# Two paddings of 32 bytes in SBUF ahead of the expert buffers of a fused attention and mixture-of-experts kernel

## The chip, the cores and the metric

The kernel runs on one core of one Trainium2 chip. The metric is the device time of one execution in microseconds (us), median of three runs.

## The reference, cut to what matters

```python
# attention: B=4, H=8, S=768, D=64; 4 sink keys and a window of 128, causal
scores = np.where(is_sink | in_window, q @ k.T / 8, -1e9)
x = softmax(scores) @ v                  # turned to (N=3072, DM=512)
# mixture of experts: E=8, F=1024, each token goes to its top 2 experts
noisy = x @ w_gate + log1p(exp(x @ w_noise)) * noise
top2, top2_w = two largest of noisy, softmax over the two
for e in range(8):
    h = relu(x[rows of e] @ w1[e])       # 512 -> 1024
    out[rows of e] += top2_w * (h @ w2[e])   # 1024 -> 512
```

All inputs and the output are float32.

## The kernel before, in words

The first stage is attention. It takes 16 pairs of heads one after the other; keys and queries of a pair land in a ring of three buffers `kq`. Scores are matmuls of line 600 into PSUM, ACT takes the exponentials into `cbuf`, TensorE transposes them (line 657), ACT or DVE copies them to `CT` (POOL makes the masked copy `CM`), and lines 682 and 685 multiply them by the values. The results are transposed, scaled and written to `x_rows` in HBM; the router (`logits`, `routing`) picks the experts meanwhile.

The second stage computes the experts one after the other on up to 832 (experts 0 to 3) or 768 rows each. Every float32 operand is split into a high and a low part (both float32r), and a product is three matmuls: high by high, high by low, low by high.

- Expert 0 multiplies up in lines 1259 to 1261 (stationary `wr`, and `hb` for the last quarter; moving `xe`, 512 columns, and `hb`, 320 columns) and down in lines 1530 to 1536.
- Experts 1 to 7 multiply up by a scheme with seven products for eight, lines 1660 to 1662 in `seven`. The stationary operand is a block of 128 columns of the weights in `wr`. The moving operand is a block of rows of 416 columns (experts 1 to 3) or 384 (4 to 7). The low parts of the rows (line 1661), and the high parts of the last products, lie in `x7`, which the profile writes as `x`; the high parts of the first four products lie in `xe`. `hb` takes the result.
- They multiply down in line 1691 (1694 for a half tile), `down7`. The stationary operand is a block of 128 columns of `hb`; the moving operand is a block of 512 columns of the weights `w2`. Chunks 0 and 1 of these weights (parts f = 0 to 3 of the sum) lie in `w2a`, chunks 2 and 3 (f = 4 to 7) in `w2b`.

Each of these matmuls loads its own stationary operand (PEld). The weights come from HBM into the ring `st`; ACT writes the high part (lines 1331 and 1372) and DVE the low part (line 503). Rows are gathered by POOL's indirect DMAs into `sg`, loaded to `xg` and transposed by DVE (line 1414). Results leave with an accumulating indirect DMA (line 1554).

Every engine's order is a list written out by hand (`ORDER` for the attention, `ORDER2` for the experts), so none of it depends on what a tile's address is. A few matmuls of `one` by itself (bfloat16, line 1961) fill TensorE's time before the experts.

Tiles are placed pool by pool, one behind the other, each rounded up to 32 bytes of a partition. The pools stand in the order `consts` (entered first, small tables), `early` (`st`, `wr`, `w2a`, `sg`, `xg`, `xe`), `tail` (tables, `turned`, `strip`, `ri`, `lg`), and then the attention's own pools (`cbuf`, `kq`, `CT` and others), whose place the experts' pool `msb` (`tmp`, `x7`, `hb`, `w2b`) takes later. `experts_setup` allocates the last tiles of `consts` (lines 1162 to 1171); the tile `turned` of `tail` is allocated in `moe_kernel`, line 1977. The program's allocation lists these first bytes, here with what is left of a division by 128:

| tile | first byte | over a multiple of 128 |
|---|---|---|
| `one`, `idf` | 8320, 9344 | 0 |
| `st`, `wr`, `w2a`, `sg`, `xg`, `xe` | 12896, 21088, 49760, 66144, 70496, 74848 | 96 |
| `turned`, `strip`, `tmp`, `x7`, `hb`, `w2b` | 96832, 112192, 116032, 123456, 156736, 212032 | 64 |
| `kq`, three buffers | 131520, 137760, 144000 | 64, 32, 0 |
| `cbuf`, `pcbuf`, `vr`, `CT`, `CM`, `ps` | 117760, 130432, 156672, 164864, 175104, 174080 | 0 |
| `vn` | 150240 | 96 |

The blocks that one expert matmul reads lie at multiples of 128 bytes from their tile's first byte (512 bytes for a stationary block, 1664 from one block of rows to the next, 2048 for `w2`, 6912, 3584 and 512 in `hb`), so all blocks of a tile stand over a multiple of 128 by the same number as the tile.

Of the kernel before, what the change touches and what calls it, by code (L numbers as in the profile page):

```python
# [9 lines left out]
F32 = mybir.dt.float32  # L10
# [399 lines left out]
def view(region, o, shape, dt):  # L410

    n = math.prod(shape[1:]) * (2 if dt in (F16, BF) else 4) // 4
    x = region[:shape[0], o:o + n].bitcast(dt)
    if len(shape) < 3:
        return x
    names = "abcd"[:len(shape) - 1]
    return x.rearrange(f"p ({' '.join(names)}) -> p {' '.join(names)}", **dict(zip(names, shape[1:])))
# [71 lines left out]
def constants(nc, pool, sh):  # L489
    c = {}  # L490
    c["one"] = pool.tile([128, 128], BF, name="one")
    nc.vector.memset(c["one"], 1.0)
    c["nz"] = pool.tile([128, sh.T, sh.E], F32, name="nz")
    jp = c["nz"].rearrange("p t e -> p (t e)")[:, :128].bitcast(I32)
    nc.gpsimd.iota(jp, pattern=[[1, 128]], base=0, channel_multiplier=-1)
    c["idf"] = pool.tile([128, 128], F32, name="idf")
    nc.vector.tensor_scalar(c["idf"], jp, 0.0, None, op0=OP.is_equal)
    c["jp"] = jp
    return c
# [369 lines left out]
def gate_loads(nc, plan, cst, sh, w_gates, noise):  # L869
    c, wbd = cst, cst["wbd"]  # L870

    def load():
        nc.sync.dma_start(wbd.rearrange("p g h i e -> p (g h i e)"), w_gates)
        nc.sync.dma_start(c["nz"].rearrange("p t e -> p (t e)"), noise)

    c["gates"] = lambda: plan.dma(2, load, 2.5, r=[("xrow", 0)], w=[("rc", 0)], n=2)
# [285 lines left out]
def experts_setup(nc, cst, sh, pool):  # L1162
    c = cst
    c["idg"] = pool.tile([128, sh.TE], I32, name="idg")
    c["idx"] = pool.tile([128, sh.E, sh.TE], I32, name="idx")
    c["at"] = {}
    c["own"] = pool.tile([128, 4], F32, name="own")
    nc.vector.tensor_tensor(c["own"], c["io"][:, :4], c["quad"].to_broadcast([128, 4]), op=OP.is_equal)
    c["pick"] = [pool.tile([128, 4, sh.E], F32, name=f"pick{i}") for i in range(2)]
    c["spacer"] = pool.tile([1, 1], F32, name="spacer")  # L1170
    c["wc"] = [pool.tile([128, sh.TE], F32, name=f"wc{i}") for i in range(2)]


def row_tile(sh, e, t):
# [720 lines left out]
def banks(*regions):  # L1895
    held = {}

    def get(i, shape, dt):
        if shape is not None:
            held[i] = view(regions[i % len(regions)], 0, shape, dt)  # L1900
        return held[i]

    return get
# [20 lines left out]
def carried(plan, sh):  # L1924
    return [(kx, plan.wrote[kx][-1]) for kx in [("lgs", (sh.B - 1) * sh.S // 256 + i) for i in range(sh.S // 256)] + [(x, 0, t) for x in ("xh", "xl") for t in range(sh.FA)]]


def phase_two(tc, nc, plan, cst, sh, w1, w2, xbuf, out):

    b, NT = sh.B - 1, sh.S // 128  # L1930
    plan.rings.update(lg=1, lt=1, lm=1, old=1, X=1, h=9)

    def turned():
        nc.gpsimd.iota(plan.get("y", -3, [128, 128], F32).rearrange("p (s i) -> p s i", i=4), pattern=[[1, 32], [32, 4]], base=0,
                       channel_multiplier=-1, allow_small_or_imprecise_dtypes=True)

    def is_one():
        g = plan.get("y", -3, [128, 128])
        nc.vector.tensor_scalar(g, g, 0.0, None, op0=OP.is_equal)

    plan.op("Pool", .4, -150, turned, w=[("y", -3)], u=[("old", 0)])
    plan.op("DVE", .2, -150, is_one, w=[("y", -3)], u=[("old", 0)])
    for _ in routing(nc, plan, cst, sh, b, 0, NT, -200, xbuf):
        pass
    experts(tc, plan, cst, sh, w1, w2, xbuf, out)


@with_exitstack
def moe_kernel(ctx, tc, sh, qk_t, v, vsink, w_gates, noise, w1c, w2c, w1, w2, out):
    nc = tc.nc  # L1950
    ctx.enter_context(tc.manual_schedule())
    xbuf = nc.dram_tensor("x_rows", (sh.N + 128, sh.XW), F32).ap()
    xsort = nc.dram_tensor("x_sorted", (sum(-(-n // 128) for n in sh.CAPS[1:]), 4, 128, sh.SW), F32).ap()
    consts = ctx.enter_context(tc.tile_pool(name="consts", bufs=1))
    early = ctx.enter_context(tc.tile_pool(name="early", bufs=1))
    cst = constants(nc, consts, sh)
    cst["xsort"] = xsort

    def ones(x):
        one = cst["one"]  # L1960
        nc.tensor.matmul(x.rearrange("p (a f) -> p a f", f=128), one, one[:, None, :].to_broadcast([128, 4, 128]), start=True, stop=True)

    with ExitStack() as both:
        tail = both.enter_context(tc.tile_pool(name="tail", bufs=1))
        with ExitStack() as st:
            flat = both.enter_context(tc.tile_pool(name="flat", bufs=1, space=bass.MemoryType.PSUM))
            bank = [flat.tile([128, 512], F32, name=f"B{i}") for i in range(4)]
            scores = st.enter_context(tc.tile_pool(name="scores", bufs=1, space=bass.MemoryType.PSUM))
            cst["S"] = [scores.tile([128, 2, 512], F32, name=f"S{i}") for i in range(2)]
            for s in cst["S"]:  # L1970
                for a in range(2):
                    nc.vector.memset(s[:64, :, a * sh.HALF + sh.NS + 192:a * sh.HALF + sh.NS + 256], 0.0)
                nc.vector.memset(s[64:, :, sh.HALF + 2 * sh.NS:sh.HALF + 3 * sh.NS], 0.0)
            routing_setup(nc, consts, tail, cst, sh)
            experts_setup(nc, cst, sh, consts)
            pools = {"tail": tail, "early": early}
            turned = tail.tile([128, 5 * sh.S], F32, name="turned")

            strip = tail.tile([128, 768], F32, name="strip")

            def of_pair(g, shape, dt):
                return turned[:, g % 5 * sh.S:(g % 5 + 1) * sh.S]

            ac = st.enter_context(tc.tile_pool(name="ac", bufs=1))
            sb = st.enter_context(tc.tile_pool(name="asb", bufs=1))
            ps = st.enter_context(tc.tile_pool(name="aps", bufs=1, space=bass.MemoryType.PSUM))
            plan = Plan(nc, {"sb": sb, "ps": ps, **pools}, {"st": 2, "w1": 4, "w2a": 2, "xg": 2, "sg": 2, "wc": 2, "xe": 1, "wr": 1, "x7": 1},
                        COLD)
            plan.laid.update(P=banks(bank[0]), X=banks(*bank[1:]), xtn=of_pair, xr=lambda n, shape, dt: view(strip, n % 3 * 256, [128, 2, 2, sh.D], F32))
            gate_loads(nc, plan, cst, sh, w_gates, noise)  # L1990
            phase_one(tc, nc, plan, ac, tail, cst, sh, qk_t, v, vsink, w1c, w2c, xbuf, out)

            plan.in_order(ORDER, (WARM, 1.2, .22, lambda: ones(bank[3])))
            live = {kx: t for kx, t in plan.live.items() if kx[0] in ("lg", "st", "wr", "w2a", "ri", "xg", "sg", "xe")}
        sb = both.enter_context(tc.tile_pool(name="msb", bufs=1))
        ps = both.enter_context(tc.tile_pool(name="mps", bufs=1, space=bass.MemoryType.PSUM))
        p2 = Plan(nc, {"sb": sb, "ps": ps, **pools}, {kx: plan.rings[kx] for kx in ("st", "xtn", "ri", "xg", "sg")})
        p2.rings.update(hb=1, x7=1, wr=1, xe=1, tmp=1)
        p2.live.update(live)
        lay_out(p2, sh, turned, of_pair, strip)  # L2000
        k = (plan.count["X"] + 1) % 3
        near = [bank[1 + (k + i) % 3] for i in range(3)]
        p2.laid.update(H=banks(near[0], bank[0]), X=banks(near[1]), TX=banks(near[2]))
        p2.count["st"] = plan.count["st"]
        past = carried(plan, sh)
        p2.follow(plan, past)
        late = max(plan.start[i] + plan.ops[i][1] for kx, i in past if kx[0] in ("xh", "xl")) - plan.free["PE"]
        for i in range(int(late / .22)):
            p2.op("PE", .22, -1000, lambda: ones(p2.get("Y", 0, [128, sh.DM], F32, "ps")))
        phase_two(tc, nc, p2, cst, sh, w1c, w2c, xbuf, out)  # L2010
        p2.in_order(ORDER2)
    spill(tc, cst, sh, w1, w2, xbuf, out)
# [23 lines left out]
```

## Time and profile before

| | |
|---|---|
| median of three runs (lowest, highest) | 705.89 us (705.38, 706.15) |
| the profiled execution: span from first to last instruction | 703.6 us |
| TensorE matmul busy (share of the span) | 689.7 us (98%) |
| TensorE weight load busy | 586.8 us (83%) |
| VectorE (DVE), ScalarE (ACT), GpSimd (POOL) busy | 521.2, 401.0, 256.3 us |
| mean granted TensorE clock | 0.998 of full speed |

The profile gives one execution's span; 2.3 us of the median lie outside it. A matmul's row shows the time from its start to the modelled end of its results, so consecutive matmuls overlap in it: a mean of 395 ns goes with starts some 230 ns apart. What a run of matmuls costs is seen from their start times.

### The profile page before, as it was taken

How to read it: one execution, taken by the hardware profiler on the slowest of the kernel's cores; microseconds unless marked ns; L12 is line 12 of the kernel's file. 1: busy time of each engine (PE TensorE's matmuls, PEld its weight loads, DVE VectorE, ACT ScalarE, POOL GpSimd, SP SyncE). 2: the span in 40 equal slices, each digit the busy share in tenths (PEclk: the TensorE clock that was granted, in tenths of full speed). 3: DMA queues.
4: the chain of work that ended last, by engine and by line, in shares of the span. 5: the costliest groups of instructions: out<-in, count | busy, mean ns of one | idle time of the engine just before them, and what ended most of it. 6: DMA issues, size and time to landing. Idle time of an engine off the chain costs nothing.

```text
span 703.6 us, 13582 instructions
## 1 busy us (share of the span) xinstructions
PE 689.7 (98%) x4759; PEld 586.8 (83%) x4759; DVE 521.2 (74%) x1268; ACT 401.0 (57%) x1119; POOL 256.3 (36%) x408
## 2 busy tenths in 40 slices
PE   8999999989999999999999999999999999999995
PEld 4777777767888999899889988998899889889984
DVE  6889999878538887959786878577877948785620
ACT  6999998853225555555546456454566545545430
POOL 3447685780335215333241233251323312021223
PEclk9999999999999999999999999999999999999999
DMA  7777786873399988475756484668857566324515
GB/s 258 237 211 253 199 238 224 246 200 89 100 295 272 254 256 232 109 199 134 215 107 205 129 202 112 189 157 223 184 141 193 130 198 123 122 67 99 119 16 77
DMA packets 87336, 123.41 MB, mean 175 GB/s; under 512 B 18656, under 2 KB 55392, under 8 KB 87264
## 3 DMA queue, kind: packets, MB, share of 16 engines
q1 hardware_dynamic: 75712, 94.51, 44.2%
q0 software_dynamic: 11408, 27.86, 20.1%
q8 instruction: 38, 0.62, 0.4%
q14 instruction: 34, 0.28, 0.1%
q10 hardware_dynamic: 144, 0.13, 0.1%
HBM read 81.75 MB, written 40.73 MB: 174 GB/s over the span
## 4 chain that ended last, share of the span: by engine, by line
PE 88%; ACT 4%; POOL 2%; DVE 2%; issue 2%; DMA 1%; SPq 0%; POOLq 0%; DVEq 0%; ACTq 0%
PE Y L1691 32%; PE B L1661 10%; PE B L1660 10%; PE B L1662 10%; PE S L600 4%; PE B L682 2%; ACT cbuf L621 2%; PE B L657 2%; PE B L1259 2%; PE B L1260 2%; PE B L1261 2%; PE Y L1530 2%; PE Y L1531 2%; PE Y L1532 2%; PE Y L1694 2%
## 5 line engine op out<-in xcount | busy, mean ns | idle before, releaser
L1661 PE MATMUL B<-x,wr 128*128 128x384 f32 (+1 forms) x392 | 134.7, 344 | 0.0
L1691 PE MATMUL Y<-w2a,hb 128*128 128x512 f32 x504 | 132.5, 395 | 0.0
L1691 PE MATMUL Y<-w2b,hb 128*128 128x512 f32 x504 | 125.9, 391 | 0.0
L1691 PEld LDWEIGHTS Y<-w2b,hb 128*128 128x128 f32 x504 | 94.4, 188 | 19.2
L1691 PEld LDWEIGHTS Y<-w2a,hb 128*128 128x128 f32 x504 | 94.1, 188 | 17.7
L1554 POOL DMA_INDIRECT out<-tmp,idx x34 | 57.9, 1703 | 118.2 <-ACT tmp L1539 105.2
L1661 PEld LDWEIGHTS B<-x,wr 128*128 128x128 f32 x392 | 73.6, 188 | 3.9
L1660 PE MATMUL B<-xe,wr 128*128 128x384 f32 (+1 forms) x224 | 76.8, 343 | 0.0
L1662 PE MATMUL B<-xe,wr 128*128 128x384 f32 (+1 forms) x224 | 76.6, 342 | 0.0
L1372 ACT ACTIVATE wr<-st 128x512 fp32r<-128x512 f32 x84 | 52.6, 627 | 36.8 <-DVE st L503 33.1
L621 ACT ACTIVATE cbuf<-S,nb 128x132 f32<-128x132 f32 x192 | 68.8, 380 | 0.6
L503 DVE TENSOR_TENSOR wr<-st,wr 128x512 fp32r<-128x512 f32 (+1 forms) x86 | 59.6, 693 | 9.4 <-ACT wr L1372 9.1
L1554 POOL DMA_INDIRECT out<-turned,idx x17 | 29.0, 1704 | 93.7 <-ACT turned L1539 89.3
L1660 PE MATMUL B<-x,wr 128*128 128x384 f32 (+1 forms) x168 | 57.8, 344 | 0.0
L1662 PE MATMUL B<-x,wr 128*128 128x384 f32 (+1 forms) x168 | 57.6, 343 | 0.0
L1675 ACT ACTIVATE tmp<-B 128x384 f32<-128x384 f32 (+1 forms) x56 | 27.8, 499 | 49.2 <-PE B L1662 37.7
L1678 DVE TENSOR_TENSOR strip<-B,strip 128x384 f32<-128x384 f32 (+1 forms) x28 | 16.0, 571 | 44.6 <-PE B L1662 24.8
L1208 POOL DMA_INDIRECT sg<-x_rows,rt_idi x30 | 32.3, 1078 | 34.4 <-DMA x_sorted<-sg 21.0
L1660 PEld LDWEIGHTS B<-xe,wr 128*128 128x128 f32 x224 | 42.1, 188 | 2.4
L600 PE MATMUL S<-kq 64*64 64x196 f32 (+2 forms) x768 | 41.3, 326 | 1.8 <-ACT cbuf L621 0.8
L1223 POOL COPY spacer<-hb 1x1 f32<-1x1 f32 x38 | 14.1, 370 | 79.2 <-ACT hb L1681 76.6
L1662 PEld LDWEIGHTS B<-xe,wr 128*128 128x128 f32 x224 | 42.0, 188 | 0.1
(312 smaller groups left out, 1554.5 us busy)
## 6 DMA issues: line engine op xcount, KB each, us to landing
st<-in_w1c SPq DMA_DIRECT2D x32, 512.0 KB, 4.0
st<-in_w2c SPq DMA_DIRECT2D x32, 512.0 KB, 4.4
kq<-in_qk_t SPq DMA_DIRECT2D x15, 780.0 KB, 5.5
xg<-x_sorted SPq DMA_DIRECT2D x42, 272.0 KB, 4.2
x_sorted<-sg SPq DMA_DIRECT2D x30, 272.0 KB, 4.7
out<-zt SPq DMA_DIRECT2D x31, 256.0 KB, 4.5
vn<-in_v SPq DMA_DIRECT2D x16, 384.0 KB, 4.3
x_rows<-strip SPq DMA_DIRECT2D x48, 128.0 KB, 3.3
```

Of the source, the lines that this page charges most:

```text
L503: eng.tensor_tensor(out, a, b, op=OP.subtract)
L600: nc.tensor.matmul(whole[x, h, c0:c1], kq(g)[r, KS + 128 * j + 64 * s:KS + 128 * j + 64 * s + 64], kq(g)[r, o + c0:o + c1], start=True, st ...
L621: nc.scalar.activation(C(n)[:, u], S_(n, 0, KW)[:, u // 2, u % 2], AF.Exp, scale=1.0 / math.sqrt(D), bias=get("nb", n)[:, u // 2, u % 2:u ...
L1208: nc.gpsimd.indirect_dma_start(out=stage(), out_offset=None, in_=xbuf, in_offset=bass.IndirectOffsetOnAxis(ap=cst["idw"]()[:, sh.TE * e + ...
L1372: plan.op("ACT", .03 + .255 * m, z, lambda: nc.scalar.activation(h(), src(), AF.Copy), r=[st], w=[(*key, b)] + old, u=[key, ex], lat=P2["s ...
L1554: d = nc.gpsimd.indirect_dma_start(out=out, out_offset=bass.IndirectOffsetOnAxis(ap=c["idx"][:size(e, t), e, t:t + 1], axis=0), in_=get("y ...
L1660: nc.tensor.matmul(p, wh, h, start=start and not k, stop=False, skip_group_check=True)
L1661: nc.tensor.matmul(p, wh, l, start=False, stop=False, skip_group_check=True)
L1662: nc.tensor.matmul(p, wl, h, start=False, stop=k == 1, skip_group_check=True)
L1675: nc.scalar.activation(u_of(e, k), src(), AF.Copy)
L1678: nc.vector.tensor_tensor(out(), src(), u_of(e, k), op=OP.add)
L1691: nc.tensor.matmul(p, h[:, x * (CAP + R) + 128 * t:x * (CAP + R) + 128 * t + 128], w[:, y], start=(f == 0 and x + y == 0), stop=(f == FC - ...
```

## The change

Two tiles of 8 float32 per partition (32 bytes) are allocated and never used: one at the end of `consts`, one in `tail` just ahead of `turned`.

```diff
@@ experts_setup
     c["wc"] = [pool.tile([128, sh.TE], F32, name=f"wc{i}") for i in range(2)]
+    pool.tile([128, 8], F32, name="to_64")
@@ moe_kernel
             pools = {"tail": tail, "early": early}
+            tail.tile([128, 8], F32, name="to_64")
             turned = tail.tile([128, 5 * sh.S], F32, name="turned")
```

All of `early` and the tables of `tail` move up by 32 bytes, and `turned` and everything behind it by 64. `st`, `wr`, `w2a`, `sg`, `xg`, `xe` go from 96 over a multiple of 128 to 0; `turned`, `strip`, `tmp`, `x7`, `hb`, `w2b` from 64 to 0; `kq` from 64, 32, 0 to 0, 96, 64; `cbuf`, `pcbuf`, `vr`, `CT`, `CM`, `ps` from 0 to 64; `vn` from 96 to 32. No instruction, order, wait or transfer changes but for these addresses.

## Rows read from the trace of the kernel before

**Rows 1.** The page, part 1: busy us, share of the span, instructions.
```profile
PE 689.7 (98%) x4759; PEld 586.8 (83%) x4759; DVE 521.2 (74%) x1268; ACT 401.0 (57%) x1119; POOL 256.3 (36%) x408
```
**Rows 2.** Windows: stretch, length, busy us of each engine, granted clock, DMA share, GB/s.
```profile
0.00:161.40 161.40, 155.06 (x2115) 112.13 (x2116) 136.40 (x373) 135.06 (x598) 98.73 (x208) 1.00 0.74 228
161.40:252.60 91.20, 91.20 (x487) 78.28 (x485) 61.74 (x194) 34.64 (x68) 30.43 (x43) 1.00 0.73 213
252.60:691.20 438.60, 438.60 (x2141) 392.85 (x2140) 322.29 (x702) 230.59 (x452) 124.56 (x154) 1.00 0.61 151
```
**Rows 3.** Waits of PE over the span: total us, times, longest; its second longest.
```profile
PE B L1286 <- DVE xe L503: 1.0, 1, 1.0
```
**Rows 4.** The page, part 4: the chain that ended last, by engine.
```profile
PE 88%; ACT 4%; POOL 2%; DVE 2%; issue 2%; DMA 1%; SPq 0%; POOLq 0%; DVEq 0%; ACTq 0%
```
**Rows 5.** Groups by shape, PE, line 1691: count, busy us, mean ns, idle.
```profile
L1691 PE MATMUL Y<-w2a,hb 128*128 128x512 f32 x504 | 132.5, 395 | 0.0
L1691 PE MATMUL Y<-w2b,hb 128*128 128x512 f32 x504 | 125.9, 391 | 0.0
```
**Rows 6.** Timeline of PE near the end: start us, us, what, count.
```profile
675.85 8.34 PE L1691 MATMUL Y<-w2b,hb 128*128 128x512 f32 x36
684.02 2.26 PE L1691 MATMUL Y<-w2a,hb 128*128 128x512 f32 x9
686.12 0.86 PE L1691 MATMUL Y<-w2b,hb 128*128 128x512 f32 x3
686.82 0.86 PE L1691 MATMUL Y<-w2a,hb 128*128 128x512 f32 x3
```
**Rows 7.** Groups by shape, PE, lines 1660 to 1662 and 1259.
```profile
L1661 PE MATMUL B<-x,wr 128*128 128x384 f32 x224 | 75.6, 338 | 0.0
L1661 PE MATMUL B<-x,wr 128*128 128x416 f32 x168 | 59.1, 352 | 0.0
L1662 PE MATMUL B<-xe,wr 128*128 128x384 f32 x128 | 43.2, 337 | 0.0
L1660 PE MATMUL B<-xe,wr 128*128 128x384 f32 x128 | 43.1, 337 | 0.0
...
L1660 PE MATMUL B<-xe,wr 128*128 128x416 f32 x96 | 33.7, 351 | 0.0
L1662 PE MATMUL B<-xe,wr 128*128 128x416 f32 x96 | 33.5, 349 | 0.0
...
L1660 PE MATMUL B<-x,wr 128*128 128x416 f32 x72 | 25.4, 353 | 0.0
L1662 PE MATMUL B<-x,wr 128*128 128x416 f32 x72 | 25.3, 351 | 0.0
...
L1259 PE MATMUL B<-hb,wr 128*128 128x320 f32 x24 | 7.5, 313 | 0.0
...
L1259 PE MATMUL B<-hb 128*128 128x320 f32 x8 | 2.5, 308 | 0.0
```
**Rows 8.** The chain that ended last in order of time: start us, us, what, count.
```profile
45.38 0.82 PE S L600 x16
...
55.18 0.82 PE S L600 x16
...
63.76 0.82 PE S L600 x16
...
161.43 1.29 PE Y L1961 x6
```
**Rows 9.** Groups by shape, ACT (line 1331) and DVE (line 503): w2a and w2b.
```profile
L1331 ACT ACTIVATE w2a<-st 128x1024 fp32r<-128x1024 f32 x16 | 16.9, 1056 | 0.1
L1331 ACT ACTIVATE w2b<-st 128x1024 fp32r<-128x1024 f32 x16 | 16.9, 1055 | 0.0
...
L503 DVE TENSOR_TENSOR w2b<-st,w2b 128x1024 fp32r<-128x1024 f32 x16 | 19.4, 1215 | 0.7 <-ACT w2b L1331 0.6
L503 DVE TENSOR_TENSOR w2a<-st,w2a 128x1024 fp32r<-128x1024 f32 x16 | 19.4, 1215 | 3.3 <-ACT w2a L1331 3.3
```

## The prediction

> **What bounds the kernel now.** I read the page first, then the windows, PE's waits, the groups by shape and the order of time. The page has PE busy for 98% of the span [rows 1], but such a share says nothing of how closely the matmuls follow each other, so the stages come next. From 161.4 to 691.2 us, where the experts are computed, PE is busy in all of both windows at the full granted clock [rows 2], and it waits for nobody there: its last wait that is worth a line is line 1286's 1.0 us, for expert 0's rows, ahead of that stage [rows 3]. The chain that ended last is 88% PE [rows 4]. So 530 of the span's 703.6 us are nothing but matmuls at the pace at which one can follow the other (2628 records by the two windows, 2584 of them products of the experts by the kernel's loops), and a change that touches no instruction can move the time only through that pace, or through the 161.4 us of attention before it, where the four other engines share the chain.
>
> What the reader is to see next is that this pace differs between matmuls of one line and one shape. Line 1691's take a mean of 395 ns with `w2a` as the moving operand and 391 ns with `w2b`, 504 of each [rows 5]. The starts say the same: 36 of `w2b` from 675.85 to 684.02 us are 8.17 us, 227 ns each, and the 9 of `w2a` behind them to 686.12 are 2.10 us, 233 ns each [rows 6]. Both are weights that the same two instructions write and that meet the same `hb`. By the table of places, what differs is the address: `w2b` and `hb` both stand at 64 over a multiple of 128, `w2a` at 96.
>
> A second pair tells which sort of address it is. In the products up, the stationary `wr` stands at 96. There the moving `xe`, at 96 too, has 351 and 349 ns with 416 columns, and `x7`, at 64, has 352, 353 and 351 [rows 7]. So it isn't that 96 is bad and 64 is good, as it was with `hb`: the slower one is each time the one whose moving and stationary operands stand at different places. With 384 columns it is 338 against 337 [rows 7], and expert 0's 320 columns have 313 ns with unlike operands (`hb` by `wr`) and 308 with like ones (`hb` by `hb`) [rows 7].
>
> **The change part by part.** The two paddings put all of these tiles at 0, so every pair of operands of the expert stage becomes a like pair. I price each unlike group by the like group of the same shape.
> - `w2a` by `hb`, 512 columns: 504 in line 1691 [rows 5], and by the kernel's loops 104 more of this kind in expert 0 and the half tiles, 608 in all, at 395 - 391 = 4 ns: 2.4 us. The starts of the last tiles would give 6 ns [rows 6], 3.8 us; the groups hold all matmuls, so I take them and keep 3.8 as an end.
> - `x7` by `wr`, 416 columns: 168 + 72 + 72 = 312 at 352 - 350 = 2 ns: 0.6 us [rows 7].
> - `x7` by `wr`, 384 columns: 224 of line 1661 and 192 of the two other lines, 416 at 1 ns at most: 0.4 us [rows 7]. The low end is nothing.
> - `hb` by `wr`, 320 columns: 24 at 5 ns, 0.1 us [rows 7]; the other unlike pairs of expert 0 are too few to count.
> - `w2b` by `hb`, `xe` by `wr`: like pairs before and after, nothing.
>
> Sum: 3.6 us less of PE in a stage in which PE's pace is the time. Is it kept? After 161.4 us PE has no wait to uncover, and DVE, the next busiest, has 61.7 of 91.2 and 322.3 of 438.6 us [rows 2]; 0.7% faster matmuls don't bring it to its limit. What would be late first is a result of ACT or DVE that now just comes in time; I count nothing for it, and at most 1 us. The end, an accumulation and two transfers behind the last matmul, only moves.
>
> ACT and DVE write `w2a` at 96 and `w2b` at 64 in 1056 and 1055 ns, 1215 and 1215 ns [rows 9]: for them an address costs nothing, so I count nothing for all that they read and write. Transfers into `st`, `xg` and `sg` land at other addresses too; PE waits for none in the expert stage, so a gain there is worth nothing and a loss would first have to outgrow the prefetch.
>
> The attention's tiles move the other way: `CT`, `cbuf`, `vr` leave a multiple of 128 for 64 over it, and the three `kq` buffers change places. The sixteen score matmuls from 45.38, 55.18 and 63.76 us read `kq` buffers at 32, 64 and 0, and take 0.82 us each time [rows 8]. So I take nothing; the far end is the 4 ns of rows 5 for each of the 2115 matmul records of that stage [rows 2], 8.5 us.
>
> The profiled execution's span of 703.6 us becomes 700.0; the timed median lies 2.3 us above that span and is taken to do so again: 705.9 - 3.6 = 702.3 us.
>
> **A rule that speaks against it.** The Trainium skill, "TensorE: Matmul & The Clock Gate", Part 2, says that TensorE has two independent SBUF read ports, so that loading the next weights takes no read bandwidth from the running matmul; by that, how one operand's address stands to the other's can't matter, and the time stays. "SBUF — State Buffer", Specifications, gives lines of 16 bytes, on whose bounds all these tiles begin before as after: the same answer. The 395 and 391 ns above disagree with both, as far as they are due to addresses.
>
> **The rivals.**
> 1. *Nothing happens: 705.9.* `w2a` and `w2b` differ in more than their place: `w2a` always holds the first half of the sum, `w2b` the second, and in the products up `x7` holds the low parts. If that is what makes the 4 and 2 ns, no address helps. For it: 1 ns at 384 columns is hardly anything, and three `w2b` in turn with `w2a`, from 686.12 to 686.82 us [rows 6], take 233 ns each like their neighbours. Against it: two pairs of tiles with opposite places agree, in groups of a hundred and more.
> 2. *The multiple of 128 itself counts: 690.* The six matmuls of `one` by itself, 512 columns with both operands at 0, start 215 ns apart (1.29 us for 6) [rows 8], against 227 and 233 [rows 6]. If the rest of that distance is due to places at 64 and 96 as well, 12 to 18 ns go, some 13 for each of 2584 matmuls: 34 us, 672. Half of it, 17 us, gives 689, say 690. Against it: `one` is bfloat16, half the bytes, and like pairs at 64 and at 96 exist and neither comes near 215.
> 3. *Slower: 710.8.* Attention's matmuls lose their multiple of 128 and pay what the experts' unlike pairs pay. At 4 ns for 2115 records this is 8.5 us, and 8.5 - 3.6 = 4.9 us more than before. It decides from 3.6 us / 2115 = 1.7 ns a record. Against it: the three equal 0.82 us, and only part of that stage's chain is PE. With no gain from the experts it would be 714.4.
>
> **How the numbers follow.** Forecast 0.60, with its own range of 700.5 (3.8 for `w2a` and all other terms doubled, about 5.4 together) to 704.5 (half of `w2a`'s term and nothing else, with some of it lost to waits); rival 1 has 0.20, rival 2 has 0.12 for anything beyond 8 us, rival 3 has 0.08. The measurement can tell 0.2%, 1.4 us, from no change. Faster is rival 2 and the forecast but for 0.03: 0.69. The same is rival 1 with that 0.03, less a little for small losses: 0.22. Slower is rival 3 and these: 0.09. The range takes in rival 1 with its spread and the nearer part of rival 2: 696 to 707.
>
> **What would show it.** Right: line 1691's two groups have the same mean, near 391, and starts of `w2a` 227 to 229 ns apart; lines 1660 to 1662 have the same mean with `x7` and `xe`, near 350 and 337; the window of the experts is 3 to 4 us shorter, and that of the attention within 0.5 us of 161.4. Wrong: `w2a` still 4 ns behind `w2b` (rival 1); `w2b` and `xe` faster than before as well, towards 215 ns at 512 columns (rival 2); line 600's sixteen over 0.82 us and a longer first window (rival 3); or new waits of PE behind 161.4 us that give the gain back.

## The result and the profile after

The changed kernel takes 700.26 us in the median of five runs (700.15 to 700.87), the kernel before, run beside it, 706.02 (705.38 to 706.36): a ratio of 0.9918, with a 95% interval of 0.9905 to 0.9931. The span of the profiled execution went from 703.6 to 698.6 us, 5.0 us less; the medians differ by 5.8. The two differ because the traced execution of the kernel before was a quick one: wherever the time and the span of one execution are both on record, they lie 1.5 to 1.8 us apart (700.26 and 698.6 for the changed kernel, 706.02 and 704.3 for one execution of the kernel before). By that a span of 703.6 belongs to a time of some 705.3, and what lies outside a span is some 1.7 us and not 2.3. All workings below go by the 5.0 of the traces. The kernel is faster by 0.8%, as forecast, and inside the whole range of 696 to 707; it is 0.2 us below the forecast's own range of 700.5 to 704.5. The gain is some one and a half times the 3.6 us of the sum.

First part 1 of the page after, which answers to [rows 1], and its part 4, which answers to [rows 4].

```profile
PE 684.9 (98%) x4759; PEld 586.4 (84%) x4759; DVE 521.3 (75%) x1268; ACT 400.5 (57%) x1119; POOL 257.1 (37%) x408
...
PE 90%; ACT 4%; DVE 2%; POOL 2%; issue 1%; POOLq 0%; ACTq 0%; DVEq 0%
```

Each engine has as many instructions as before. PE's busy time fell by 4.8 us; that of the others moved by less than 1. The windows after (columns as in [rows 2]):

```profile
0.00:161.40 161.40, 155.35 (x2115) 112.32 (x2116) 136.39 (x374) 134.75 (x598) 98.95 (x208) 1.00 0.75 228
161.40:252.60 91.20, 91.20 (x490) 78.75 (x488) 61.98 (x195) 35.21 (x70) 30.75 (x43) 1.00 0.73 213
252.60:691.20 438.60, 438.33 (x2158) 395.37 (x2156) 322.33 (x703) 230.55 (x452) 126.39 (x156) 1.00 0.60 152
```

The attention's window holds the same 2115 matmul records, and the first matmul of the experts starts at the same time (162.37 before, 162.35 after). In the two windows of the experts more records fit into the same stretch, 490 for 487 and 2158 for 2141: the same stream, packed closer. The clock is full in all of them, so the pace is not the clock's. PE's waits after have nothing behind the one of [rows 3], which is still 1.0 us:

```profile
PE B L1287 <- DVE xe L503: 1.0, 1, 1.0
```

Now the groups by shape that answer to [rows 5, 7] (the lines stand one further down: 1692 was 1691, 1661 to 1663 were 1660 to 1662, 1260 was 1259):

```profile
L1692 PE MATMUL Y<-w2a,hb 128*128 128x512 f32 x504 | 130.1, 390 | 0.0
L1692 PE MATMUL Y<-w2b,hb 128*128 128x512 f32 x504 | 124.9, 390 | 0.0
L1662 PE MATMUL B<-x,wr 128*128 128x384 f32 x224 | 75.3, 336 | 0.0
L1662 PE MATMUL B<-x,wr 128*128 128x416 f32 x168 | 58.9, 351 | 0.0
...
L1661 PE MATMUL B<-xe,wr 128*128 128x384 f32 x128 | 43.3, 338 | 0.0
...
L1661 PE MATMUL B<-xe,wr 128*128 128x416 f32 x96 | 33.8, 352 | 0.0
L1663 PE MATMUL B<-xe,wr 128*128 128x416 f32 x96 | 33.3, 347 | 0.0
L1661 PE MATMUL B<-x,wr 128*128 128x416 f32 x72 | 25.4, 352 | 0.0
L1663 PE MATMUL B<-x,wr 128*128 128x416 f32 x72 | 25.0, 347 | 0.0
...
L1260 PE MATMUL B<-hb,wr 128*128 128x320 f32 x24 | 7.4, 310 | 0.0
```

The 395 of `w2a` against the 391 of `w2b` is gone: 390 each. `x7` and `xe` with 416 columns have equal means now, line by line: 352 and 352 on line 1661, 347 and 347 on line 1663. And PE in the order of time near the end, which answers to [rows 6]:

```profile
669.77 0.39 PE L1692 MATMUL Y<-w2a,hb 128*128 128x512 f32 x1
669.99 0.33 PE L1661 MATMUL B<-x,wr 128*128 128x384 f32 x1
...
671.04 8.33 PE L1692 MATMUL Y<-w2b,hb 128*128 128x512 f32 x36
679.21 2.20 PE L1692 MATMUL Y<-w2a,hb 128*128 128x512 f32 x9
681.25 0.84 PE L1692 MATMUL Y<-w2b,hb 128*128 128x512 f32 x3
681.93 0.84 PE L1692 MATMUL Y<-w2a,hb 128*128 128x512 f32 x3
...
683.97 2.20 PE L1692 MATMUL Y<-w2b,hb 128*128 128x512 f32 x9
686.01 2.20 PE L1692 MATMUL Y<-w2a,hb 128*128 128x512 f32 x9
```

The 36 of `w2b` still start 227 ns apart (8.17 us), but the 9 of `w2a` now do so as well (2.04 us, 227; they took 233). The row at 681.25 is the one to look at: three `w2b` in turn with `w2a` take 0.68 us, 227 ns each, where [rows 6] had 0.70, 233 each. Their own operands were alike before as well. So it is with the nine `w2b` from 683.97: 2.04 us, 227 each, where the trace before has 2.08, 231 each:

```profile
688.90 2.24 PE L1691 MATMUL Y<-w2b,hb 128*128 128x512 f32 x9
690.98 1.33 PE L1691 MATMUL Y<-w2a,hb 128*128 128x512 f32 x5
```

A mean in a group is the duration of a matmul up to its modelled end. What PE's time consists of is the distance from one start to the next. Summed over the whole trace, each distance counted for the matmul that starts it:

| moving operand by stationary, columns | matmuls | ns before | ns after | us less |
|---|---|---|---|---|
| `w2a` by `hb`, 512 | 608 | 232.8 | 228.1 | 2.85 |
| `w2b` by `hb`, 512 | 607 | 229.5 | 227.5 | 1.18 |
| `x7` by `wr`, 416 | 312 | 190.0 | 188.3 | 0.53 |
| `x7` by `wr`, 384 | 416 | 175.2 | 174.7 | 0.23 |
| `xe` by `wr`, 416 | 192 | 187.6 | 186.9 | 0.14 |
| `xe` by `wr`, 384 | 256 | 175.3 | 175.6 | -0.08 |
| `xe` by `hb`, 512 (expert 0) | 24 | 241.3 | 236.9 | 0.10 |
| `hb` by `wr`, 320 (expert 0) | 72 | 147.8 | 147.0 | 0.06 |

These make the 5.0 us; all the rest between PE's first and last start, the attention and expert 0's like pairs included, has 184.02 and 183.97 us. Two terms carry it: the predicted one, and 1.18 us of `w2b`, which was counted at nothing.

What is left above 227 ns in the changed kernel has an order too. Behind a product up of 416 columns the products down start 226 to 227 ns apart from the first on. Behind one of 384 columns the first few take longer, with all operands alike by 128: in the mean 230.6, 234.8, 228.3, 231.4 and 230.3 ns for `w2a` in the first five places of a run, 231.8 and 232.2 for `w2b` in the first two, and 226.5 to 226.8 from the sixth place on. One such run, six `w2b` behind 384 columns, takes 1.38 us, 230 each:

```profile
666.70 0.34 PE L1663 MATMUL B<-x,wr 128*128 128x384 f32 x1
666.88 1.55 PE L1692 MATMUL Y<-w2b,hb 128*128 128x512 f32 x6
668.26 0.33 PE L1661 MATMUL B<-xe,wr 128*128 128x384 f32 x1
```

### The profile page after: what moved, and what is told of

Its sections match the earlier page's. It is cut to its first block, busy times and chain, and to the rows that moved or that the text cites. A ratio compares the mean times of both kernels' runs of the same rounds, so it can differ in the third digit from the quotient of the medians.

```text
span 698.6 us, 13582 instructions
## 1 busy us (share of the span) xinstructions
PE 684.9 (98%) x4759; PEld 586.4 (84%) x4759; DVE 521.3 (75%) x1268; ACT 400.5 (57%) x1119; POOL 257.1 (37%) x408
## 4 chain that ended last, share of the span: by engine, by line
PE 90%; ACT 4%; DVE 2%; POOL 2%; issue 1%; POOLq 0%; ACTq 0%; DVEq 0%
PE Y L1692 32%; PE B L1661 10%; PE B L1662 10%; PE B L1663 10%; PE S L600 4%; PE B L682 3%; ACT cbuf L621 2%; PE B L657 2%; PE B L685 2%; PE B L1260 2%; PE B L1261 2%; PE B L1262 2%; PE Y L1531 2%; PE Y L1532 2%; PE Y L1533 2%; PE Y L1695 2%
## 5 line engine op out<-in xcount | busy, mean ns | idle before, releaser
L1692 PE MATMUL Y<-w2a,hb 128*128 128x512 f32 x504 | 130.1, 390 | 0.0
```

The lines of the kernel that those rows point to most:

```text
L1692: nc.tensor.matmul(p, h[:, x * (CAP + R) + 128 * t:x * (CAP + R) + 128 * t + 128], w[:, y], start=(f == 0 and x + y == 0), stop=(f == FC - ...
```

## The experiments

Two theories stood against each other after the result. A: the moving and the stationary operand must stand alike over a multiple of 128 bytes. B: they must stand on a multiple of 128 (or 64) itself. After the change both hold. Each time below is a median beside runs of the kernel before on the same chip; "over" means over a multiple of 128.

**One padding alone, the second.** All the experts' tiles stand at 96 over: alike, none on a multiple of 128, 64 or anything above 32.

```diff
+            tail.tile([128, 8], F32, name="to_64")
             turned = tail.tile([128, 5 * sh.S], F32, name="turned")
```

> The second padding alone: the early tiles (wr, w2a, xe) stay at 96 over a multiple of 128, the later ones (x7, hb, w2b) go from 64 to 96, so all operands of the experts are like pairs but none is at a multiple of 128 or of 64. Theory A (what counts is that the moving and the stationary operand stand alike): the whole gain, 700.3 us, within 1 us; w2a and w2b at 390 ns each, starts of w2a 228 ns apart. Theory B (a multiple of 64 or 128 itself counts): no gain or slower, 705 to 708, with w2b as slow as w2a was, 394 to 395 ns.

Measured: 700.25 us against 705.62, ratio 0.9926 (0.9913 to 0.994), span 699.1. The groups of the products down:

```profile
L1691 PE MATMUL Y<-w2a,hb 128*128 128x512 f32 x504 | 130.1, 390 | 0.0
L1691 PE MATMUL Y<-w2b,hb 128*128 128x512 f32 x504 | 124.9, 389 | 0.0
```

All of the gain comes with this one padding, with every tile of the experts off a multiple of 64. B falls.

**The other padding alone.** `st`, `wr`, `w2a`, `xe` at 0, `x7`, `hb`, `w2b` at 96: a multiple of 128 for half of the tiles, and the same pairs unlike as before.

```diff
     c["wc"] = [pool.tile([128, sh.TE], F32, name=f"wc{i}") for i in range(2)]
+    pool.tile([128, 8], F32, name="to_64")
```

> The first padding alone: the early tiles (wr, w2a, xe) go to 0 over a multiple of 128, the later ones (x7, hb, w2b) to 96. The pairs are as unlike as before the change (apart by 32 of 128). Theory A: no gain, 706 us, within 1 us; w2a at 394 to 395 ns. Theory B: about half the gain or more, 702 to 704, since w2a, wr and xe now begin at a multiple of 128.

Measured: 705.71 us, ratio 0.9999 (0.999 to 1.0008), span 704.5. The groups are those of [rows 5], 395 and 391:

```profile
L1692 PE MATMUL Y<-w2a,hb 128*128 128x512 f32 x504 | 132.5, 395 | 0.0
L1692 PE MATMUL Y<-w2b,hb 128*128 128x512 f32 x504 | 125.9, 391 | 0.0
```

**All at 64.** Paddings of 96 and 32 bytes put every tile of the experts at 64 over.

```diff
+    pool.tile([128, 24], F32, name="to_64")
...
+            tail.tile([128, 8], F32, name="to_64")
```

> Paddings of 96 and 32 bytes: all tiles of the experts stand at 64 over a multiple of 128, like pairs everywhere. Theory A: the whole gain, 700.3 us, within 1 us. If the multiple of 128 is what made w2b's spacing fall from 229.5 to 227.5 ns though its pair was like before as after, w2b stays at 229 and the time is about 1.2 to 2 us longer, 701.5 to 702.3.

Measured: 700.39 us, ratio 0.9928 (0.9915 to 0.9942), span 698.7; starts 228.2 ns apart with `w2a`, 227.5 with `w2b`, as in the changed kernel. Places 0, 64 and 96 give one time as long as they are shared.

**Apart by 64.** The same two sizes the other way round: early tiles at 0, later ones at 64.

```diff
+    pool.tile([128, 8], F32, name="to_64")
...
+            tail.tile([128, 24], F32, name="to_64")
```

> Paddings of 32 and 96 bytes: the early tiles at 0 over a multiple of 128, the later ones at 64, so the unlike pairs are apart by 64 instead of 32. If being alike counts by multiples of 128: as slow as before, 706 us or more. If it counts by multiples of 64: the whole gain, 700.3 us. Theory B for multiples of 64 says 700.3 as well, so this one is read together with the run in which everything stands at 96.

Measured: 705.74 us, ratio 1.0 (0.9991 to 1.0009), span 704.2.

```profile
L1692 PE MATMUL Y<-w2a,hb 128*128 128x512 f32 x504 | 132.6, 395 | 0.0
L1692 PE MATMUL Y<-w2b,hb 128*128 128x512 f32 x504 | 125.7, 391 | 0.0
```

All places are multiples of 64 here and nothing is gained: 64 bytes apart is as bad as 32. So alike counts by 128 or by a multiple of it. Which one, these runs do not separate: by the first bytes in the table of places, the operands down that are alike by 128 are alike by 256 as well in every one of the kernels, and two operands down 128 bytes apart were not tried.

What was left open by these four is the size, above all why `w2b` gained. Two ways: a slow matmul also delays the ones around it (carry), or `w2b` had something of its own.

**Down all unlike, up alike.** From the changed kernel: `hb` moved to 32 over, everything else kept at 0 (the second size makes the 32 up to 128).

```diff
@@ Plan.get, at a tag's first tile
+            if tag in ("hb", "w2b") and not any(k[0] == tag for k in self.live):
+                self.pools["sb"].tile([128, 8 if tag == "hb" else 24], F32, name=f"apart_{tag}")
```

> The changed kernel with hb moved up by 32 bytes and w2b kept over a multiple of 128: the products up (wr by xe and x7) stay like pairs, all 1216 products down are apart by 32 of 128, also those of w2b that were alike before the change. Theory A: the products down cost what w2a's cost before, 232.8 instead of 227.8 ns, 1216 x 5 = 6.1 us, so 706.3 us, with line 1692's two groups at 394 to 395 ns and the products up unchanged. If w2b's groups had gained by something else than the stand of the two operands, w2b stays at 390 and the time is 703.3.

Measured: 708.95 us, ratio to the kernel before 1.005 (1.0036 to 1.0064), span 707.4, 8.8 us over that of the changed kernel. (The few products of expert 0 that read `hb` on the way up are unlike here too.)

```profile
L1694 PE MATMUL Y<-w2a,hb 128*128 128x512 f32 x504 | 132.7, 395 | 0.0
L1694 PE MATMUL Y<-w2b,hb 128*128 128x512 f32 x504 | 128.3, 396 | 0.0
...
L1665 PE MATMUL B<-xe,wr 128*128 128x416 f32 x96 | 33.8, 352 | 0.0
...
L1663 PE MATMUL B<-xe,wr 128*128 128x416 f32 x96 | 33.7, 352 | 0.0
```

`w2b`, unlike for the first time, takes 396, and starts 234.0 ns apart: 6.5 ns over the changed kernel. The time is 2.7 us more than was expected. Part of that is in the products up, whose operands were left alike: line 1665 (1663 of the changed kernel) has 352 for 347, and all 192 matmuls of `xe` with 416 columns have 189.8 ns for 186.9 between starts.

**Down all alike, up unlike.** From the kernel before: `w2a`, `xe`, `x7`, `hb`, `w2b` at 64, `wr` left at 96.

```diff
@@ Plan.get, at a tag's first tile
+            if tag == "w2a" and not any(k[0] == tag for k in self.live):
+                self.pools["early"].tile([128, 24], F32, name="alike")
@@ moe_kernel
+            tail.tile([128, 8], F32, name="to_64")
```

> The kernel before, with w2a moved to 64 over a multiple of 128 where hb and w2b stand; in the products up all moving operands (xe too) are apart from wr by 96 of 128. The counterpart of the run above: products down alike, products up unlike. Theory A: down gains w2a's 2.9 us, up loses 0.5 us for xe at 416 columns and 0.3 us in expert 0. If w2b's 1.2 us come from the stand of w2a's matmuls among which they run (how far the weight load ahead has got), they come here as well: 702.5. If they come from the products up or from the multiple of 128, w2b stays at 229.5 ns: 703.7.

Measured: 703.17 us, ratio 0.9971 (0.9958 to 0.9983), span 701.5. Starts with `w2a` go from 232.8 to 229.2 ns, and with `w2b`, whose own places are those of the kernel before, from 229.5 to 228.1; `xe` with 416 columns, unlike now, goes from 187.6 to 190.2. So `w2b` is faster because its neighbours are. It stays 0.6 ns above the changed kernel, where the products up are alike as well. The time is 0.7 us over the 702.5 that was expected for this case.

**Only `w2a` apart.** The sharpest form of the same question: from the changed kernel, `w2a` alone moved to 32 over.

```diff
@@ Plan.get, at a tag's first tile
+            if tag in ("w2a", "sg") and not any(k[0] == tag for k in self.live):
+                self.pools["early"].tile([128, 8 if tag == "w2a" else 56], F32, name=f"apart_{tag}")
```

> The changed kernel with w2a alone moved, to 32 over a multiple of 128; w2b and every other operand of the experts stay alike, all distances else the same by 256. Theory C (a matmul hands on the moment at which the next one starts, so that a like pair among unlike ones is slower too): w2a 232.8 to 233.2 ns between starts, 608 x 4.9 = 3.0 us, and w2b at 229 instead of 227.5, 0.9 us more: 704.3 us. Against it (each pair pays by its own two addresses alone): w2b stays at 227.5 and the time is 703.3.

Measured: 705.81 us against 706.02, ratio 0.9998 (0.9989 to 1.0007), span 703.4; 1.5 us more than theory C gave. The groups by shape:

```profile
L1694 PE MATMUL Y<-w2a,hb 128*128 128x512 f32 x504 | 132.7, 395 | 0.0
L1694 PE MATMUL Y<-w2b,hb 128*128 128x512 f32 x504 | 125.8, 391 | 0.0
...
L1663 PE MATMUL B<-xe,wr 128*128 128x416 f32 x96 | 33.8, 352 | 0.0
L1665 PE MATMUL B<-xe,wr 128*128 128x416 f32 x96 | 33.6, 350 | 0.0
```

And PE in order of time near the end:

```profile
675.65 8.35 PE L1694 MATMUL Y<-w2b,hb 128*128 128x512 f32 x36
683.84 2.26 PE L1694 MATMUL Y<-w2a,hb 128*128 128x512 f32 x9
685.94 0.86 PE L1694 MATMUL Y<-w2b,hb 128*128 128x512 f32 x3
686.63 0.85 PE L1694 MATMUL Y<-w2a,hb 128*128 128x512 f32 x3
```

`w2a`'s 16 KB a partition, moved by 32 bytes, give all of the gain back. `w2a`'s own starts explain 5.1 ns by 608, 3.1 of the 4.8 us between the spans; `w2b`, at the same place as in the changed kernel, has 229.1 for 227.5 (1.0 us), `xe` with 416 columns 188.8 for 186.9 (0.4 us), `x7` 0.7 ns more with 416 and with 384 columns (0.5 us) and `xe` with 384 0.8 ns (0.2 us). That is 5.2 us; 0.4 of them are hidden in the spans, because the experts' first matmul happens to start that much earlier here, at 161.97 us. The order of time shows where: 36 of `w2b` on end have 227.5 ns (8.19 us), three of them between `w2a` take 0.69 us, 230 each. A long row of like matmuls is hardly touched; one that stands among unlike ones is.

**Sixteen bytes.** From the changed kernel, `hb` is used from its fifth number on, 16 bytes further.

```diff
-    return plan.get("hb", 0, [128, 8 * (2 * CAP + 64)], F32R, "sb")
+    return plan.get("hb", 0, [128, 8 * (2 * CAP + 64) + 64], F32R, "sb")[:, 4:4 + 8 * (2 * CAP + 64)]
```

> The changed kernel with hb begun 16 bytes into its tile: products down apart by 16 bytes of 128, a distance that whole tiles cannot have. If any distance costs the full price: 706.3 us. If the price grows with the distance up to 32: 703 or so. If 16 bytes are within one unit of what is read at a time: 700.3.

Measured: 705.17 us, ratio 0.9995 (0.9986 to 1.0004), span 703.6.

```profile
L1692 PE MATMUL Y<-w2a,hb 128*128 128x512 f32 x504 | 131.8, 394 | 0.0
L1692 PE MATMUL Y<-w2b,hb 128*128 128x512 f32 x504 | 127.2, 394 | 0.0
```

Starts are 231.3 and 231.8 ns apart, between the 228.1 and 227.5 of no distance and the 233.2 and 234.0 of 32 bytes: some two thirds of the price. Sixteen bytes, the only distance below 32 that was tried, is not free.

**Is the rest of the distance above 215 ns due to places too?** Rival 2 rested on `one` by itself, 215 ns in bfloat16 with both operands at 0 [rows 8]. This kernel makes those six matmuls twenty-four of ones as float32r, moving operand at 0, stationary at 0 (alike) or 32 bytes on (apart); some 4 us of its time are the added matmuls.

```diff
...
+            nc.tensor.matmul(x.rearrange("p (a f) -> p a f", f=128), one[:, apart:apart + 128], one[:, None, :128].to_broadcast([128, 4, 128]), start=True, stop=True)
...
```

> The changed kernel in which the six matmuls of ones ahead of the experts are 24 of four-byte operands (float32r), 512 columns, the first twelve with moving and stationary operand at the same place, the next twelve with the stationary one 32 bytes further; some 4 us are added to the kernel, which its time here shows and which is of no interest. Theory A: starts 227 ns apart in the first twelve and 231 to 235 in the others, so that what is left over the 215 ns of the two-byte matmuls goes with the four-byte operands and not with places. If places at a multiple of 128 gave 215 (rival 2 of the prediction), the first twelve are 215 to 218 ns apart.

Measured: 704.15 us in a single run, span 702.6. The hand-written order takes them as 8 apart, 8 alike, 4 apart, 4 alike, not twelve and twelve. From the chain in order of time, in four stretches (start us, us, what, count):

```profile
161.33 1.86 PE Y L1970 x8
163.19 1.36 PE Y L1970 x6
164.55 1.39 PE Y L1970 x6
165.94 0.46 PE Y L1970 x2
```

That is 232, 227 and 232 ns each, with 227 and 226 between the starts of the last stretch. So a float32r matmul of 512 columns starts 227 ns after the one before it with both operands at one place on a multiple of 128: the 12 ns above 215 go with the type of the operands, and a shared place does not take them away. Rival 2 falls. The same starts hold the carry by itself: after the last apart one the next two starts are still 232 and 231 ns apart before 227 comes back, though all of the operands are alike again. The first slow start is the first apart one's own, 235 ns after the alike one ahead of it. But the step from the last of the ones to the experts' first products, from like operands to like ones, does it too: 233 and 231 ns, then 226. So unlike places are not the only thing that leaves two slow starts behind it.

**Does it count by 256 as well?** In the changed kernel's trace, the matmuls of `xe` with 416 columns (blocks 1664 bytes, 6.5 times 256, apart) have 184.6 ns between starts where block and weights stand alike by 256, and 189.1 where they are 128 apart; with 384 columns 174.5 and 176.6. (The expectation has 190.9 and 177.5, which do not fit the means of 186.9 and 175.6 over halves of equal number.) The blocks 128 apart are no group of their own either: of the six matmuls of a product, three on the first block and three on the second, the first on the second block has 195.0 ns and the last 183.2. This kernel puts `xe`'s blocks, and `x7`'s with 384 columns, at multiples of 256.

```diff
...
-    t = plan.get("x7", 1, [128, 20 * WIDE], F32R, "sb").rearrange("p (b w) -> p b w", w=WIDE)
-    h = plan.get("xe", 0, [128, 4096])[:, :8 * WIDE].rearrange("p (b w) -> p b w", w=WIDE)
+    w = CAPS[e] // 2
+    t = plan.get("x7", 1, [128, 20 * WIDE], F32R, "sb")[:, :20 * w].rearrange("p (b w) -> p b w", w=w)
+    h = plan.get("xe", 0, [128, 4128])[:, :8 * 448].rearrange("p (b w) -> p b w", w=448)
...
```

> The changed kernel with the blocks of rows laid at multiples of 256 bytes from each other where there is room: xe's blocks 448 columns apart instead of 416, x7's 384 apart for the experts with 384 columns. In the trace of the changed kernel the blocks that stand 128 bytes off by 256 are slower (xe with 416 columns 190.9 against 184.6 ns between starts, with 384 177.5 against 174.4). If being alike counts by 256: xe's second blocks gain 96 x 6 + 128 x 3 = 1.0 us and x7's 384 about 0.2, so 699.1 us. If it counts by 128 alone, those differences are of the order of the loops and nothing changes: 700.3.

Measured: 702.31 us, ratio 0.9956 (0.9942 to 0.997), span 700.5: 1.9 us over the changed kernel, where a gain was hoped for. All 192 matmuls of `xe` with 416 columns stand alike by 256 now and have 188.0 ns, not 184.6:

```profile
L1664 PE MATMUL B<-xe,wr 128*128 128x416 f32 x96 | 33.6, 350 | 0.0
L1662 PE MATMUL B<-xe,wr 128*128 128x416 f32 x96 | 33.6, 350 | 0.0
```

A split read out of one trace did not carry over to another arrangement, and what makes the 12 ns between the six matmuls of a product is open. What this kernel lost lies for the most part in the products down, whose places were not changed: `w2a`'s starts went to 229.4 ns and `w2b`'s to 228.3. They are slower right behind the products up of 416 columns, where `w2a` now takes 230.9, 232.9 and 230.4 ns in the first three places of a run (226.7, 226.8 and 226.7 in the changed kernel). So a new arrangement of the products up is carried into the products down, though the operands of both are alike by 128. With 384 columns, where all blocks stand alike by 256 here, the mean of `x7` and `xe` is 174.9 ns after 175.0, so there 128 bytes between them cost nothing that can be seen; but 32 bytes cost only half a nanosecond there.

## Why the prediction was right, and where its sum was short

- *What bounds the kernel.* Right: with PE's pace as the time, the 5.0 us between the starts are the 5.0 us between the spans. No wait gave any of it back, and the at most 1 us set aside for that was not needed.
- *Like pairs, not good places.* Right, and this was the step that mattered: it was read from two pairs of tiles with opposite places [rows 5, 7]. The kernels with all tiles at 96, at 64 and at 0 take the same time, and those 32 or 64 apart the old one. There was some luck in it: the first pair, 395 and 391, was a solid sign, but the second was not. In the changed kernel, with all operands alike, the means of lines 1661 and 1663 differ by 5 ns (352 and 347), so 1 or 2 ns between groups of those lines could not tell a place from a position in the order.
- *`w2a` at 4 ns, 2.4 us.* Right in kind; it is 4.7 ns and 2.85 us. The difference of the means, 4 ns, was too small and the 6 ns of the last starts [rows 6] too large (608 by 6 ns is 3.6 us; the 3.8 set down for it would be 6.25 ns). All starts of the trace before would not have done better: 232.8 against 229.5 is 3.3 ns, because `w2b`, the yardstick, was slowed itself.
- *`w2b` by `hb` and `xe` by `wr`: nothing.* This is the step that failed. `w2b` gave 1.18 us, `xe` by `wr` some 0.1. A like matmul behind unlike ones is slowed as well. In the trace before, the first seven `w2b` behind a `w2a` start 233.4, 231.4, 229.8, 232.5, 231.3, 229.7 and 229.9 ns apart in the mean, and the later ones 226.8; in the changed kernel all of these are 226.4 to 227.0. So the like group that served as the yardstick was itself a mixture, and each comparison of it with the unlike group came out too small. It is shown from both sides: `w2a` alone put apart slows `w2b` by 1.6 ns, and making `w2a` and `hb` alike without touching `w2b` and `hb` speeds it up by 1.4.
- The evidence was in rows that the prediction did quote, for rival 1: three `w2b` in turn with `w2a` take 233 ns, 36 on end 227 [rows 6]. It was taken as a hint that the place doesn't matter; it was the neighbours. Priced at the clean row of 227 ns, 608 of `w2a` at 5.8 and 607 of `w2b` at 2.5 would have been 5.0 us for the products down, nearer to the 4.0 measured than 2.4.
- *`x7`: 0.6 and 0.4.* 0.53 and 0.23; 320 columns 0.1, measured 0.06. The sizes came out, though the means that they were read from could not carry 1 and 2 ns (above).
- *Attention moves nothing.* Right: same records in the window, the sixteen scores still 0.82 us, e.g. from 45.42, 55.21 and 63.77 us, and the rest of PE the same to 0.05 us. Rival 3 falls. Why that stage's pairs show no price was not looked into.
- *The signs.* They came as listed (390 and 390; `w2a` at 228.1 ns; equal means line by line with 416 columns; the first window unchanged), but for a stage shorter by 5.0 us and not 3 to 4, and for `w2b`, faster by 2.0 ns, which had been set down as a sign of rival 2. It was none: `w2b` has the same 227.5 ns with all tiles at 64.
- *The range.* The forecast's own lower end doubles all terms but `w2a`'s and calls that 5.4 us together; 3.8 and twice 0.6, 0.4 and 0.1 are 6.0, which gives 699.9, and 700.26 would have been inside. Its upper end names half of `w2a`'s term, 1.2 us, which gives 704.7 and not 704.5.
- *Rival 1, nothing happens,* falls with the result, and with it what the two rules of the Trainium skill would give. The Trainium skill, "TensorE: Matmul & The Clock Gate", Part 2, has independent read ports for weights and moving data; here one tile moved by 32 bytes makes 233 ns of 228, by how the places of the two operands stand to each other. The Trainium skill, "SBUF — State Buffer", Specifications, has lines of 16 bytes; here 16 bytes more in one operand cost 3.2 and 4.3 ns a matmul. By the measurements distances of 16, 32 and 64 bytes cost, whatever else the rules hold for.
- *Outside the span.* The prediction carried 2.3 us over to the changed kernel. That figure was the median of three runs less the span of one quick execution; an execution's time lies some 1.7 us above its own span, before and after. Medians of the kernel before lay between 705.5 and 706.0 over the chips used.

Why the distance between the two operands matters inside the chip is not shown by any of these runs, and no story for it is offered.

## What to carry to other kernels

Where matmuls of float32r with 512 columns, each with its own weights, follow each other without a wait, look up the first byte of the moving and the stationary tiles and give all pairs the same remainder by 128 (the like pairs down shared it by 256 here, so that is the safe choice); 32 bytes of padding ahead of one pool were enough, and it made no difference whether the remainder was 0, 64 or 96. With 384 columns there was next to nothing to gain. Compare such a pace by distances between starts, within long rows of one kind: a group that is interleaved with slow matmuls is no clean yardstick, and a price taken against it is too low. And cure all of the interleaved pairs: here `w2a` left apart kept all of the loss.

## What the runs showed of the hardware that was not expected

- How far a moving operand stands from a stationary one, by the remainders of their first bytes by 128, sets 227 to 228 or some 233 ns for a float32r matmul of 512 columns; 16 bytes cost about two thirds of what 32 do, and 64 as much as 32.
- A slow matmul's effect outlasts it: with ones in all operands two starts more at 231 to 232 ns before 227 returns, and some seven like `w2b` behind a `w2a` that is apart. A change from one kind of product to another can do the same with all operands alike: the first two to five products down behind products up of 384 columns take 228 to 235 ns in the changed kernel.
- With ones by ones, both operands at one place on a multiple of 128, float32r has 227 ns where bfloat16 has 215 for the same 512 columns.
- Within the changed kernel, matmuls of one shape on the same block of `xe` with 416 columns differ by 12 ns by their position in the order (195.0 and 183.2); the one arrangement of blocks that was tried made the kernel slower.
